# Exp straight from the score PSUM, a check of the row sums in place of the max pass, and another access order for the query copies, in a grouped-query attention kernel

## The chip, the cores and the metric

The kernel runs on one core of a Trainium2 chip. The metric is the time of one execution on the device in microseconds (us), and lower is better. "Median" is the median of several executions. The "span" is the length of the one execution that the profiler recorded; in these runs it is 1.7 to 3.6 us shorter than the time of that same execution. Some executions are flagged slow: they lie over 1.5% above the fastest of their kernel.

## The reference, cut to what matters

```python
B, Hq, Hkv, Sq, Sk, D = 16, 32, 8, 16, 2048, 128
# q, k, v: bfloat16, normal * 0.05
k = jnp.repeat(k, rep, axis=1)          # rep = Hq // Hkv = 4
v = jnp.repeat(v, rep, axis=1)
scores = jnp.einsum("bhqd,bhkd->bhqk", q, k) * D ** -0.5
p = softmax(scores, axis=-1)
return jnp.einsum("bhqk,bhkd->bhqd", p, v)
```

There are 128 heads of K and V (16 batches times 8). Each serves 4 x 16 = 64 rows of queries. The kernel works on pairs of heads, so that a tile has 128 rows, and there are 64 pairs. A pair needs two heads of K and two of V, 512 KB each. In all the core moves 138.43 MB by its data queue. The inputs are small, so the scores lie near zero and every row sum of the exponentials lies near 2048.

## The kernel before: the parts that matter

The kernel is a static program. A list scheduler in Python, run while the kernel is built, puts the operations of each engine in an order, from a table of durations. On the chip nothing is decided any more: each engine runs its list in order and waits on semaphores. In the code and the views PE is TensorE, PEld its loading of weights, DVE VectorE, ACT ScalarE, POOL GpSimd, and SPq the queue of SyncE that issues the DMA transfers. Names that end in _ps lie in PSUM, the memory that TensorE writes its results to; the other tiles lie in SBUF.

```python
# operations of pair p (engine): what each waits for
# kx  DVE       KT <- Kn      transposes K in 32x32 blocks      (K landed)
# qt  PE        QT_ps <- Qr   transposes a quarter of a chunk of queries
# qe  ACT       QT <- QT_ps   copies it out, interleaving the rows
# S   PE        S_ps <- KT,QT scores, 128 x 2048 f32, one buffer
# mx  DVE       Sneg <- S_ps  negate, scale, and take the row minimum on the way
# ex  ACT       P <- Sneg     exp with the bias nbias; its accumulator is the row sum
# pt  PE        PT_ps <- P    two halves; pe (ACT or DVE) copies each out
# pv  PE        O_ps <- PT,V
# rc, nm, ST    1/rowsum, scaling, store
add(("S", p), ("kx", 2 * p), ("kx", 2 * p + 1), ..., opt(p >= 1, ("mx", p - 1)))
add(("mx", p), ("S", p), opt(p >= 2, ("ex", p - 2)))
add(("ex", p), ("mx", p), ...)
...
_ENGS = {"kx": ("dve",), "mx": ("dve",), "nm": ("act", "dve"), "pe": ("act", "dve"), "qe": ("act",), ...}
...
elif kind == "mx":
    ins = eng.tensor_scalar(Sneg[p % 2][:, :], S_ps[:, :], -scale, None,
                            op0=ALU.mult, op1=ALU.min, accum_out=nbias[:, p:p + 1])
elif kind == "ex":
    ins = eng.activation(P[...], Sneg[p % 2][...], ACT.Exp,
                         bias=nbias[:, p:p + 1], scale=-1.0, accum_out=rowsum[:, p:p + 1])
...
if kind == "qe":                      # NI = 8
    dst = QT[p % 2][:, op[2], :].rearrange("d (a i) -> d i a", i=NI)   # store: step of 8 bf16 = 16 bytes
    src = QT_ps[:, 0:qch].rearrange("d (i a) -> d i a", i=NI)          # read: one after the other
ins = eng.activation(dst, src, ACT.Copy) if me == "act" else eng.tensor_copy(dst, src)
```

A chunk of queries serves eight pairs and needs four copies "qe". All loads and stores stand in one queue, in order; K runs two pairs ahead of V.

Of the kernel before, what the change touches and what calls it, by code (L numbers as in the profile page):

```python
# [6 lines left out]
ALU = mybir.AluOpType  # L7
# [5 lines left out]
NBV = 14  # L13
# [6 lines left out]
QLEAD = 5  # L20

# [4 lines left out]
    ("dve", "pe"): 0.69, ("act", "pe"): 1.03, ("act", "qe"): 1.06, ("act", "nm"): 0.42,  # L26
# [10 lines left out]
         "qe": ("act",), "qr": ("pool",), "ex": ("act",), "qt": ("pe",), "S": ("pe",), "pt": ("pe",), "pv": ("pe",)}  # L37
# [3 lines left out]
def make_ops(NP, pairs_per_chunk):  # L41
# [23 lines left out]
    for p in range(NP):  # L65
        add(("S", p), ("kx", 2 * p), ("kx", 2 * p + 1), *[("qe", ch(p), x) for x in range(4)],
            opt(p >= 1, ("mx", p - 1)))
        add(("mx", p), ("S", p), opt(p >= 2, ("ex", p - 2)))
        add(("ex", p), ("mx", p), *[opt(p >= 2, ("pt", p - 2, h)) for h in range(2)])
        for h in range(2):  # L70
            add(("pt", p, h), ("ex", p), opt(p >= 1, ("pe", p - 1, h)))
            add(("pe", p, h), ("pt", p, h), opt(p >= NPT, ("pv", p - NPT)))
        add(("pv", p), ("pe", p, 0), ("pe", p, 1), ("V", 2 * p), ("V", 2 * p + 1), opt(p >= 1, ("nm", p - 1)))
        add(("rc", p), ("ex", p))
        add(("nm", p), ("pv", p), ("rc", p), opt(p >= NBO, ("ST", p - NBO)))
        add(("ST", p), ("nm", p))
# [20 lines left out]
def build_schedule(NP, pairs_per_chunk):  # L97

    deps, dma = make_ops(NP, pairs_per_chunk)
# [51 lines left out]
def bass_standalone__gqa_softmax__sampling_kernel(  # L151
# [36 lines left out]
    rowsum = sb("rowsum", [128, NP], F32)  # L188
    rrec = sb("rrec", [128, NP], F32)
# [8 lines left out]
    sem_eng = {e: sem(f"sem_{e}") for e in ("pe", "dve", "act", "pool")}  # L198
    rings = {"K": NBK, "V": NBV, "Q": 2, "ST": NBO}
    sem_dma = {kind: [sem(f"sem_{kind}{i}") for i in range(n)] for kind, n in rings.items()}  # L200

    deps, progs, _ = build_schedule(NP, qch // 128)
    where = {}
    for e in ("pe", "dve", "act", "pool"):
        for i, op in enumerate(progs[e]):
            where[op] = (e, i + 1)
# [6 lines left out]
    def wait_point(op):  # L213
        if op[0] in rings:
            n = rings[op[0]]
            return sem_dma[op[0]][op[1] % n], 16 * (op[1] // n + 1)
        e, i = where[op]
        return sem_eng[e], i

    def make_waiter(eng, me):  # L220
        seen = {}

        def waits(op):
            need = {}
            for d in deps[op]:
                if me == "pe" and d in where and where[d][0] == "pe":
                    continue
                s, n = wait_point(d)
                key = s.name
                if n > max(seen.get(key, 0), need.get(key, (None, 0))[1]):  # L230
                    need[key] = (s, n)
            for key, (s, n) in need.items():
                seen[key] = n
                eng.wait_ge(s, n)

        return waits

    def elementwise(eng, me):
        waits = make_waiter(eng, me)
        for op in progs[me]:  # L240
# [12 lines left out]
            elif kind == "ex":  # L253
                ins = eng.activation(  # L254
                    P[p % 2][:, :].rearrange("m (r a j) -> m a r j", a=4, j=32),
                    Sneg[p % 2][:, :].rearrange("m (a r j) -> m a r j", a=4, j=32), ACT.Exp,
                    bias=nbias[:, p:p + 1], scale=-1.0, accum_out=rowsum[:, p:p + 1])
            elif kind == "rc":
                ins = eng.reciprocal(rrec[:, p:p + 1], rowsum[:, p:p + 1])  # L259
            elif kind == "nm":  # L260
                dst, src, r = Osb[p % NBO][:, :], O_ps[:, 0:128], rrec[:, p:p + 1]
                if me == "act":
                    ins = eng.activation(dst, src, ACT.Copy, scale=r)  # L263
                else:
                    ins = eng.tensor_scalar(dst, src, r, None, op0=ALU.mult)  # L265
            else:
                if kind == "qe":
                    dst = QT[p % 2][:, op[2], :].rearrange("d (a i) -> d i a", i=NI)
                    src = QT_ps[:, 0:qch].rearrange("d (i a) -> d i a", i=NI)
                else:  # L270
                    h = op[2]
                    dst = PT[p % NPT][:, 8 * h:8 * (h + 1), :]
                    src = PT_ps[h][:, :].rearrange("k (t m) -> k t m", t=8)
                ins = eng.activation(dst, src, ACT.Copy) if me == "act" else eng.tensor_copy(dst, src)  # L274
            ins.then_inc(sem_eng[me], 1)

    with nc.Block() as block:  # L277

        @block.gpsimd
        def _(gp):  # L280
            gp.iota(iota_t[:, :], [[1, 128]], base=0, channel_multiplier=-1).then_inc(sem_id, 1)
            gp.wait_ge(sem_id, 1)
            gp.tensor_scalar(ident[:, :], iota_t[:, :], 0.0, None, op0=ALU.is_equal).then_inc(sem_id, 1)
            elementwise(gp, "pool")

        @block.sync
        def _(sp):
            waits = make_waiter(sp, "sp")
            for op in progs["sp"]:
                kind, x = op  # L290
                waits(op)
                s = x % rings[kind]
                if kind == "K":
                    dst, src = Kn[s][:, :].bitcast(BF16), kf[x].rearrange("(a j) d -> a (j d)", j=J)
                elif kind == "V":
                    dst, src = Vb[s][:, :, :], vf[x].rearrange("(a j) d -> a j d", j=J)
                elif kind == "Q":
                    dst, src = Qn[s][:, :, :], qf[qch * x:qch * (x + 1), :].rearrange("(a i) d -> a i d", i=NI)
                else:
                    dst, src = of[128 * x:128 * (x + 1), :], Osb[s][:, :]  # L300
                sp.dma_start(dst, src).then_inc(sem_dma[kind][s], 16)  # L301
            for p in range(max(0, NP - NBO), NP):
                sp.wait_ge(*wait_point(("ST", p)))

        @block.tensor
        def _(pe):
            waits = make_waiter(pe, "pe")
            pe.wait_ge(sem_id, 2)
            for op in progs["pe"]:
                kind, p = op[0], op[1]  # L310
                waits(op)
                if kind == "qt":
                    x = op[2]
                    for i in range(NI):
                        ins = pe.transpose(  # L315
                            QT_ps[:, 128 * i:128 * (i + 1)],
                            Qr[:, x, i, :],
                            ident[:, :],
                        )
                elif kind == "S":  # L320
                    c, pp = divmod(p, qch // 128)
                    for x in range(4):
                        for a in range(4):
                            for gg in range(2):
                                kt = KT[p % NKT][32 * a:32 * (a + 1), gg, :].bitcast(BF16)
                                kt = kt.rearrange("i (r b j e) -> i r b j e", b=2, j=32, e=2)
                                ins = pe.matmul(  # L327
                                    S_ps[64 * gg:64 * (gg + 1), 512 * a:512 * (a + 1)],
                                    QT[c % 2][32 * a:32 * (a + 1), x, 128 * pp + 64 * gg:128 * pp + 64 * (gg + 1)],
                                    kt[:, :, x // 2, :, x % 2],  # L330
                                    start=(x == 0), stop=(x == 3), tile_position=(32 * a, 64 * gg),
                                )
                elif kind == "pt":
                    h = op[2]
                    for t in range(8):
                        r = 8 * h + t
                        ins = pe.transpose(PT_ps[h][:, 128 * t:128 * (t + 1)],  # L337
                                           P[p % 2][:, 128 * r:128 * (r + 1)], ident[:, :])
                else:
                    for r in range(J):  # L340
                        for gg in range(2):
                            ins = pe.matmul(  # L342
                                O_ps[64 * gg:64 * (gg + 1), 0:128],
                                PT[p % NPT][:, r, 64 * gg:64 * (gg + 1)],
                                Vb[(2 * p + gg) % NBV][:, r, :],
                                start=(r == 0), stop=(r == J - 1), skip_group_check=True,
                            )
                ins.then_inc(sem_eng["pe"], 1)

        @block.vector  # L350
        def _(dve):
            elementwise(dve, "dve")

        @block.scalar
        def _(act):
            elementwise(act, "act")
# [28 lines left out]
```

## Time and profile before

| | before |
|---|---|
| median of the first three runs | 478.08 us (477.15 to 480.02) |
| span of the profiled run | 473.1 us |
| busiest engine | ScalarE (ACT), 381.1 us, 81% |
| copies QT<-QT_ps | 32 x 4.72 us = 151 us |
| max passes Sneg<-S_ps | 64 x 2.29 us = 147 us |
| data moved, mean rate | 138.43 MB, 293 GB/s |

The first view is the page of the kernel before: first the busy time of each engine, then, for 40 equal slices of the span (11.8 us each), the granted TensorE clock in tenths, the busy share of the DMA engines in tenths and what they moved.

```profile
PE 275.6 (58%) x5376; PEld 194.3 (41%) x5376; DVE 327.2 (69%) x369; ACT 381.1 (81%) x308; POOL 28.9 (6%) x34
...
PEclk9999877975898677966899667995579776779999
DMA  8951978995889549995599839998299972999990
GB/s 300 413 220 49 348 265 286 360 413 182 308 315 401 197 169 407 352 361 182 213 406 400 319 133 332 340 408 306 89 353 320 401 278 115 340 337 363 411 367 10
```

The DMA row is not flat. It stands at 9 for a few slices and then falls, again and again, as one chunk of queries follows another (GB/s 49, 182, 169, 182, 133, 89, 115). In many of the slices at or after a fall the granted TensorE clock is low as well (digits 5 to 7).

The groups of instructions of the kernel before name the operations. The columns are: source line, engine, operation, output<-input, shapes, count; then total busy us and mean ns of one; then the idle time before them and who ended it.

```profile
L251 DVE TENSOR_SCALAR_CACHE_REDUCE Sneg<-S_ps 128x2048 f32<-128x2048 f32 x64 | 146.5, 2289 | 66.2 <-PE S_ps L327 64.1
L274 ACT ACTIVATE QT<-QT_ps 128x1024 bf16<-128x1024 bf16 x32 | 151.1, 4723 | 13.5 <-PE QT_ps L315 13.4
L254 ACT ACTIVATE P<-Sneg,nbias 128x2048 bf16<-128x2048 f32 x64 | 129.3, 2020 | 8.8 <-DVE Sneg L251 8.6
L274 ACT ACTIVATE PT<-PT_ps 128x1024 bf16<-128x1024 bf16 x92 | 94.9, 1072 | 31.2 <-PE PT_ps L337 31.2
```

The second and the last of these lines are the ones to compare. Both are ScalarE copies of 1024 bf16 elements for each of 128 partitions out of PSUM. One takes 4.72 us, the other 1.07 us. What differs between them is the engine's access pattern. The first line is the max pass.

The windows view of the kernel before gives busy us of PE, PEld, DVE, ACT and POOL in a stretch of 10 us, with the granted clock, the DMA's share and GB/s at the end. The first stretch lies at a chunk of queries, the second does not.

```profile
220.00:230.00 10.00, 7.44 (x96) 5.47 (x96) 5.85 (x7) 9.24 (x9) 0.00 (x0) 0.53 0.05 11
440.00:450.00 10.00, 6.36 (x163) 4.55 (x160) 9.91 (x11) 8.99 (x11) 0.00 (x0) 1.00 1.03 412
```

At the chunk ScalarE is busy for 9.24 of 10 us, and the DMA falls to 11 GB/s; the granted clock is 0.53 there and 1.00 in the other stretch. Away from the chunk the DMA runs at 412 GB/s.

This is the longest of the waits of the transfer queue (total us, times, longest us):

```profile
SPq L301 <- ACT O L263: 257.6, 53, 26.2
```

The queue waits for the scaling of an output tile. Only a store waits for that, and the store of a pair stands in the same queue in front of later loads. From 215.0 to 228.2 us, for example, nothing is issued: ScalarE runs two query copies of 4.7 us (started at 213.78 and 220.18), then the scaling ends at 228.14 us and the store goes out at 228.16. Waits for a free buffer of K (<-DVE KT) come to 2.1 us in all.

### The profile page before, as it was taken

Reading aid. Unit: us, or ns where it says so; the run is one execution under the profiler, and the core shown is the slowest. Engines: PE = TensorE matmul, PEld = TensorE weight load, DVE = VectorE, ACT = ScalarE, POOL = GpSimd, SP = SyncE. Lnnn points to the kernel's source line nnn. Section 1 sums busy time; section 2 is a strip of 40 time slices with the busy share of each in tenths; the row PEclk is TensorE's granted clock in tenths of the full one; section 3 lists DMA queues with packets and bytes.
Section 4 is the critical chain, followed back from the end, with each engine's and each line's share of the span. In section 5 each row is a group of like instructions: output and inputs, shape, how many; then the busy total and the mean of one; then the engine's idle time right before and its main releaser. Section 6 shows DMA issues by size and latency. Waiting matters only on the chain.

```text
span 473.1 us, 11999 instructions
## 1 busy us (share of the span) xinstructions
PE 275.6 (58%) x5376; PEld 194.3 (41%) x5376; DVE 327.2 (69%) x369; ACT 381.1 (81%) x308; POOL 28.9 (6%) x34
## 2 busy tenths in 40 slices
PE   1147547737655566646666456654666645675754
PEld 1115435525443354433544234442544424454543
DVE  5237567936795478955799366993579645889994
ACT  6859987999499966999588993899948799479894
POOL 0200000300003000110003000030000300000000
PEclk9999877975898677966899667995579776779999
DMA  8951978995889549995599839998299972999990
GB/s 300 413 220 49 348 265 286 360 413 182 308 315 401 197 169 407 352 361 182 213 406 400 319 133 332 340 408 306 89 353 320 401 278 115 340 337 363 411 367 10
DMA packets 47282, 139.19 MB, mean 294 GB/s; under 512 B 13440, under 2 KB 13440, under 8 KB 47232
## 3 DMA queue, kind: packets, MB, share of 16 engines
q1 hardware_dynamic: 47232, 138.43, 77.9%
q8 instruction: 42, 0.69, 0.6%
q14 instruction: 8, 0.07, 0.0%
HBM read 136.31 MB, written 2.10 MB: 293 GB/s over the span
## 4 chain that ended last, share of the span: by engine, by line
issue 16%; ACT 14%; PE 12%; DVE 4%; DMA 3%; POOL 1%; SPq 1%; ACTq 0%; POOLq 0%
ACT PT L274 7%; ACT QT L274 5%; PE S_ps L327 4%; PE O_ps L342 4%; PE PT_ps L337 3%; DMA Qn<-in_q_dram 3%; ACT P L254 2%; DVE Sneg L251 1%; DVE PT L274 1%; POOL Qr L249 1%; DVE KT L244 1%; PE QT_ps L315 1%; SPq L301 1%; ACTq L277 0%; ACT O L263 0%
## 5 line engine op out<-in xcount | busy, mean ns | idle before, releaser
L251 DVE TENSOR_SCALAR_CACHE_REDUCE Sneg<-S_ps 128x2048 f32<-128x2048 f32 x64 | 146.5, 2289 | 66.2 <-PE S_ps L327 64.1
L274 ACT ACTIVATE QT<-QT_ps 128x1024 bf16<-128x1024 bf16 x32 | 151.1, 4723 | 13.5 <-PE QT_ps L315 13.4
L244 DVE STREAM_TRANSPOSE KT<-Kn 128x1024 int32<-128x1024 int32 x128 | 153.5, 1225 | 2.4 <-DMA Kn<-in_k_dram 2.3
L254 ACT ACTIVATE P<-Sneg,nbias 128x2048 bf16<-128x2048 f32 x64 | 129.3, 2020 | 8.8 <-DVE Sneg L251 8.6
L342 PE MATMUL O_ps<-Vb,PT 128*64 128x128 bf16 x2048 | 82.6, 243 | 77.1 <-ACT PT L274 69.8
L274 ACT ACTIVATE PT<-PT_ps 128x1024 bf16<-128x1024 bf16 x92 | 94.9, 1072 | 31.2 <-PE PT_ps L337 31.2
L342 PEld LDWEIGHTS O_ps<-Vb,PT 128*64 128x64 bf16 x2048 | 71.2, 125 | 92.6 <-ACT PT L274 81.9
L327 PE MATMUL S_ps<-KT,QT 32*64 32x512 bf16 x2048 | 89.5, 469 | 21.3 <-DVE KT L244 13.7
L337 PE MATMUL PT_ps<-ident,P 128*128 128x128 bf16 x1024 | 84.4, 248 | 11.8 <-ACT P L254 11.6
L337 PEld LDWEIGHTS PT_ps<-ident,P 128*128 128x128 bf16 x1024 | 72.2, 113 | 40.5 <-ACT P L254 29.0
L315 PE MATMUL QT_ps<-ident,Qr 128*128 128x128 bf16 x256 | 27.0, 270 | 84.6 <-ACT QT L274 56.7
L315 PEld LDWEIGHTS QT_ps<-ident,Qr 128*128 128x128 bf16 x256 | 20.4, 120 | 93.0 <-issue 77.6
L327 PEld LDWEIGHTS S_ps<-KT,QT 32*64 32x64 bf16 x2048 | 30.7, 120 | 49.8 <-issue 20.7
L249 POOL COPY Qr<-Qn 128x1024 bf16<-128x1024 bf16 x28 | 28.0, 1040 | 347.9 <-DMA Qn<-in_q_dram 346.7
L274 DVE COPY PT<-PT_ps 128x1024 bf16<-128x1024 bf16 x36 | 24.1, 689 | 32.1 <-PE PT_ps L337 32.0
L263 ACT ACTIVATE O<-O_ps,rrec 128x128 bf16<-128x128 f32 x53 | 20.9, 394 | 30.6 <-PE O_ps L342 30.3
L259 DVE RECIPROCAL rrec<-rowsum 128x1 f32<-128x1 f32 x64 | 9.1, 143 | 24.7 <-ACT P L254 24.6
L265 DVE TENSOR_SCALAR O<-O_ps,rrec 128x128 bf16<-128x128 f32 x11 | 3.9, 351 | 14.8 <-PE O_ps L342 14.8
L254 ACT ACTIVATION_READ_ACCUMULATOR P<-Sneg,nbias 128x1 f32 x64 | 12.5, 195 | 0.0
L251 DVE DVE_READ_ACCUMULATOR Sneg<-S_ps 128x1 f32 x64 | 5.3, 83 | 0.0
L249 DVE COPY Qr<-Qn 128x1024 bf16<-128x1024 bf16 x2 | 1.3, 690 | 3.4 <-DMA Qn<-in_q_dram 3.4
L249 ACT ACTIVATE Qr<-Qn 128x1024 bf16<-128x1024 bf16 x2 | 2.0, 1050 | 1.4 <-DMA Qn<-in_q_dram 1.4
(7 smaller groups left out, 2.5 us busy)
## 6 DMA issues: line engine op xcount, KB each, us to landing
Kn<-in_k_dram SPq DMA_DIRECT2D x128, 512.0 KB, 6.4
Vb<-in_v_dram SPq DMA_DIRECT2D x128, 512.0 KB, 8.0
Qn<-in_q_dram SPq DMA_DIRECT2D x8, 256.0 KB, 6.1
out_dram<-O SPq DMA_DIRECT2D x64, 32.0 KB, 4.7
```

The source lines that it names most:

```text
L244: ins = eng.transpose(KT[(p // 2) % NKT][:, p % 2, :], Kn[p % NBK][:, :])
L249: ins = eng.activation(dst, src, ACT.Copy) if me == "act" else eng.tensor_copy(dst, src)
L251: ins = eng.tensor_scalar(Sneg[p % 2][:, :], S_ps[:, :], -scale, None, op0=ALU.mult, op1=ALU.min, accum_out=nbias[:, p:p + 1])
L254: ins = eng.activation(P[p % 2][:, :].rearrange("m (r a j) -> m a r j", a=4, j=32), Sneg[p % 2][:, :].rearrange("m (a r j) -> m a r j", a= ...
L259: ins = eng.reciprocal(rrec[:, p:p + 1], rowsum[:, p:p + 1])
L263: ins = eng.activation(dst, src, ACT.Copy, scale=r)
L274: ins = eng.activation(dst, src, ACT.Copy) if me == "act" else eng.tensor_copy(dst, src)
L301: sp.dma_start(dst, src).then_inc(sem_dma[kind][s], 16)
L315: ins = pe.transpose(QT_ps[:, 128 * i:128 * (i + 1)], Qr[:, x, i, :], ident[:, :],)
L327: ins = pe.matmul(S_ps[64 * gg:64 * (gg + 1), 512 * a:512 * (a + 1)], QT[c % 2][32 * a:32 * (a + 1), x, 128 * pp + 64 * gg:128 * pp + 64 * ...
L337: ins = pe.transpose(PT_ps[h][:, 128 * t:128 * (t + 1)], P[p % 2][:, 128 * r:128 * (r + 1)], ident[:, :])
L342: ins = pe.matmul(O_ps[64 * gg:64 * (gg + 1), 0:128], PT[p % NPT][:, r, 64 * gg:64 * (gg + 1)], Vb[(2 * p + gg) % NBV][:, r, :], start=(r ...
```

## The change

The intent was to drop the pass that finds the row maximum. Softmax does not need it where exp can neither overflow nor vanish, so exp reads the scores straight from PSUM. For safety the kernel tests at its end that all row sums lie in 1e-18..1e18. If one does not, every engine runs a second, complete program with the max pass. The diff also turns the access order of the query copy round, and lets that copy run on VectorE too.

```diff
-         "qe": ("act",), ...
+         "qe": ("act", "dve"), ...
@@ dependencies
-            opt(p >= 1, ("mx", p - 1)))
-        add(("mx", p), ("S", p), opt(p >= 2, ("ex", p - 2)))
-        add(("ex", p), ("mx", p), ...)
+            opt(p >= 1, ("mx" if general else "ex", p - 1)))
+        if general:
+            add(("mx", p), ("S", p), opt(p >= 2, ("ex", p - 2)))
+        add(("ex", p), ("mx" if general else "S", p), ...)
@@ exp
+                src = Sneg[p % 2] if prog.general else S_ps
...
-                    bias=nbias[:, p:p + 1], scale=-1.0, accum_out=rowsum[:, p:p + 1])
+                    bias=nbias[:, p:p + 1] if prog.general else 0.0, scale=-1.0 if prog.general else scale,
+                    accum_out=rowsum[:, p:p + 1])
@@ query copy
-                    dst = QT[p % 2][:, op[2], :].rearrange("d (a i) -> d i a", i=NI)
-                    src = QT_ps[:, 0:qch].rearrange("d (i a) -> d i a", i=NI)
+                    dst = QT[p % 2][:, op[2], :].rearrange("d (a i) -> d a i", i=NI)
+                    src = QT_ps[:, 0:qch].rearrange("d (i a) -> d a i", i=NI)
@@ the end of each engine's program
+    def unless_in_range(eng, work):
+        reg = eng.alloc_register("flag")
+        eng.wait_ge(sem_flag, 4)
+        eng.reg_load(reg, flag[0:1, 0:1].bitcast(I32))
+        with eng.If_ne(reg, all_within):
+            fast.wait_stores(eng)
+            work()                      # the whole second program
@@ VectorE, after its last operation
+            for x, (bound, test) in enumerate(((LOW, ALU.is_ge), (1.0 / LOW, ALU.is_le))):
+                dve.tensor_scalar(inside[:, x, :], rowsum[:, :], bound, None, op0=test, op1=ALU.add,
+                                  accum_out=within[:, x:x + 1]).then_inc(sem_flag, 1)
+            dve.wait_ge(sem_flag, 3)    # PE has summed the counts over the partitions
+            dve.reduce_sum(flag[0:1, 0:1], QT_ps[0:1, 0:4].bitcast(F32), ...).then_inc(sem_flag, 1)
```

Since the scheduler runs again, the orders change too: 19 of the 32 query copies, 72 of the 128 PT copies (before: 36) and 58 of the 64 scalings (before: 11) now stand on VectorE.

## The prediction

> **What bounds the kernel now.** By the page's busy table ScalarE is the busiest (381.1 of 473.1 us, 81%), then VectorE (327.2), TensorE (275.6, mean clock 0.825). The groups of instructions say why: 32 copies of transposed queries, QT<-QT_ps, take 4723 ns each (151.1 us), while PT<-PT_ps, with as many elements and bytes, takes 1072 ns. Their store steps by 16 bytes per bf16 element. [...] These copies come in fours. The 40-slice table shows the damage: around each chunk of queries the DMA falls from 400–413 GB/s to 100–250 and PEclk to 0.5–0.7, and the first score matmul starts only at 28.1 us (timeline). Between chunks most 10-us windows show 390–412 GB/s, PEclk 1.0. There the timeline shows a pair of heads every 4.7 us when data is at hand, ScalarE full (exp 2.0 + 0.2, two PT copies 1.94, O 0.36).
>
> **What the change does.** It removes the 64 max passes (2289 ns + 83 = 151.8 us of VectorE) and their place in the chain S -> max -> exp. Exp reads PSUM; PT copies from PSUM (1072 ns) cost what a same-sized SBUF copy costs on ScalarE (1050), so I expect 2.0 + 0.2 us still. S_ps is now held until exp ends, so score and exp of adjacent pairs no longer overlap. The query copy's store becomes contiguous, its PSUM read strided. Instruction order moves work to VectorE: 19 of 32 query copies, 72 of 128 PT copies (was 36), 58 of 64 O scalings (was 11).
> Sums from the trace's durations, query copy assumed 1.1 us on ScalarE, 1.25 on VectorE:
> - ScalarE 64x2.2 + 56x1.05 + 13x1.1 + 6 = 220 us;
> - VectorE 128x1.225 + 72x0.69 + 58x0.35 + 64x0.14 + 19x1.25 + 1 = 261 us;
> - TensorE, warm, per pair 1.08 (S) + 1.07 (PT) + 1.08 (O).
> The serial chain of a pair, exp 2.2 -> PT_ps 1.07 -> S 1.08 -> waits 0.4, is 4.75 us.
>
> **The new bound is the DMA.** 138.43 MB at the saturated 402 GB/s (estimate: mean of the full windows of before) is 344 us, 5.35 us a pair, above the chain's 4.75 and every engine's sum. [...] the trace never passes 413. Add 3 us of ramp, about 4 for the last O, scaling and store, and 3–4 for the check at the end (two tests, a matmul, a reduction, register load, branch), partly under the store; then 2–4 for the difference between span and timed run. The fallback does not execute: every row sum should be near 2048.
>
> **Predicted: 358 us**, 350 to 380 eight times in ten; faster by over 2% 0.97, within 2% 0.02, slower 0.01.
>
> **What would show it.** DMA share near 99% in almost all slices without hollows at chunks; PEclk near 1.0; no Sneg group; QT copies 1.0–1.3 us; exp from PSUM 2.0–2.1 us; engines at about 220 (ScalarE) and 260 (VectorE); first S near 13 us; last load landing near 347 us.
>
> **What would make it wrong.** Strided PSUM reads still costing 4 us: three such copies per chunk on VectorE would push it above 5.35 us a pair (375–390 us). Exp from PSUM much slower than 2.2 us, or TensorE throttled to half clock (chain 2.2 + 2x2.15 + 0.4 = 6.9 us), would make the S–exp chain the bound. In-order stores in the load queue could stall loads early. The branch at the end could cost more than 4 us.

344 us of transfers, 3 of ramp, about 4 for the last output, 3 to 4 for the check and 2 to 4 between span and timed run come to 356 to 359 us, put at 358. Two figures had no figure of the trace behind them and were guesses: 1.25 us for a query copy on VectorE, and 3 to 4 us for the check. The runs later showed 1.19 and 3.5 us. Between span and timed run the profiled execution has 1.8 us before (474.86 - 473.1) and 1.8 after (358.22 - 356.4). "Warm" stands for a granted clock of 1.00: there the trace before has 1.08 us for the scores of a pair (start at 442.76 us), and 1.93 us in a stretch at 0.53 (start at 222.15 us).

## The result and the profile after

The changed kernel takes 359.4 us in the median of 4 runs (357.52 to 360.96), against 478.79 us for the kernel before in the same rounds. The ratio is 0.7506, with a 95% interval of 0.7456 to 0.7557. Here and below a ratio is the mean time of one kernel's fast runs over that of the other's fast runs of the same rounds, so it is not quite the ratio of the medians. The output is correct, and the second program did not run.

This is the page of the changed kernel, with the same rows as before (a slice is now 8.9 us).

```profile
PE 240.3 (67%) x5378; PEld 173.7 (49%) x5378; DVE 244.2 (69%) x348; ACT 201.1 (56%) x206; POOL 28.9 (8%) x35
...
PEclk9999998998989998989988998999989999989897
DMA  7999999999999999999999999999999999999940
GB/s 291 413 409 407 410 411 406 412 411 411 409 411 410 411 412 410 411 412 409 410 409 412 411 410 409 411 409 409 411 411 410 405 410 404 408 412 410 405 164 12
```

The DMA row is 9 from the second slice to the 38th. No fall is left. No engine of computation is busy for more than 69% of the span.

The groups of instructions after the change:

```profile
L255 DVE STREAM_TRANSPOSE KT<-Kn 128x1024 int32<-128x1024 int32 x128 | 157.5, 1232 | 14.1 <-DMA Kn<-in_k_dram 13.6
L266 ACT ACTIVATE P<-S_ps 128x2048 bf16<-128x2048 f32 x64 | 120.1, 1877 | 54.9 <-PE S_ps L326 54.7
L287 ACT ACTIVATE PT<-PT_ps 128x1024 bf16<-128x1024 bf16 x56 | 57.3, 1023 | 76.9 <-PE PT_ps L336 76.9
L287 DVE COPY PT<-PT_ps 128x1024 bf16<-128x1024 bf16 x72 | 47.4, 667 | 7.4 <-PE PT_ps L336 7.1
L287 DVE COPY QT<-QT_ps 128x1024 bf16<-128x1024 bf16 x19 | 22.7, 1194 | 1.6 <-PE QT_ps L314 1.6
L287 ACT ACTIVATE QT<-QT_ps 128x1024 bf16<-128x1024 bf16 x13 | 13.2, 1019 | 5.4 <-PE QT_ps L314 5.4
```

The query copies fell from 4723 to 1019 ns on ScalarE, and take 1194 ns on VectorE. Exp takes 1877 ns. The max pass has no line.

The chain of waits that ended last, by engine, for the changed kernel:

```profile
DMA 62%; PE 19%; ACT 8%; SPq 5%; DVE 4%; issue 2%
```

Followed back from the end, 62% of the span is waiting for a transfer. The kernel before had 3% there, but its chain could be followed over about half of its span only (its shares add up to 51%).

The windows view of the changed kernel, with one long stretch and one at the end of the stream of loads:

```profile
43.00:335.00 292.00, 202.35 (x4570) 146.47 (x4564) 206.09 (x290) 168.32 (x174) 23.93 (x24) 0.94 1.03 410
338.00:345.00 7.00, 4.58 (x122) 2.99 (x121) 4.35 (x7) 2.89 (x4) 0.00 (x0) 1.00 0.56 215
```

For 292 us the DMA moves 410 GB/s. This is the new bound. Near 338 us the DMA's busy share falls to about half, and stays there for about 7 us, before the loads are through.

The last view is the timeline of the changed kernel from 22.9 us, where data is at hand. Its columns are start, duration, engine, line, operation.

```profile
22.93 1.07 PE L336 MATMUL PT_ps<-ident,P 128*128 128x128 bf16 x16 [0.54 <-ACT P L266]
23.92 1.14 PE L326 MATMUL S_ps<-KT,QT 32*64 32x512 bf16 x32
25.14 1.88 ACT L266 ACTIVATE P<-S_ps 128x2048 bf16<-128x2048 f32 x1 [0.44 <-PE S_ps L326]
27.16 1.07 PE L336 MATMUL PT_ps<-ident,P 128*128 128x128 bf16 x16 [0.53 <-ACT P L266]
```

The transposes of P start at 22.93 and again at 27.16 us. The serial chain exp, PT, S takes 4.2 us a pair, when nothing makes it wait.

### The profile page after: what moved, and what is told of

It is laid out like the page before. It is cut to its first block, busy times and chain, and to the rows that moved or that the text cites. A ratio compares the mean times of both kernels' runs of the same rounds, so it can differ in the third digit from the quotient of the medians.

```text
span 356.4 us, 11923 instructions
## 1 busy us (share of the span) xinstructions
PE 240.3 (67%) x5378; PEld 173.7 (49%) x5378; DVE 244.2 (69%) x348; ACT 201.1 (56%) x206; POOL 28.9 (8%) x35
## 4 chain that ended last, share of the span: by engine, by line
DMA 62%; PE 19%; ACT 8%; SPq 5%; DVE 4%; issue 2%
DMA Vb<-in_v_dram 58%; PE O_ps L341 7%; ACT P L266 6%; PE PT_ps L336 6%; SPq L304 5%; PE S_ps L326 4%; DMA Kn<-in_k_dram 3%; DVE KT L255 2%; DVE PT L287 1%; ACT QT L287 1%; PE QT_ps L314 1%; DMA Qn<-in_q_dram 1%; DVE O L278 1%; ACT Qr L260 0%; DVE rrec L272 0%
## 5 line engine op out<-in xcount | busy, mean ns | idle before, releaser
L255 DVE STREAM_TRANSPOSE KT<-Kn 128x1024 int32<-128x1024 int32 x128 | 157.5, 1232 | 14.1 <-DMA Kn<-in_k_dram 13.6
L266 ACT ACTIVATE P<-S_ps 128x2048 bf16<-128x2048 f32 x64 | 120.1, 1877 | 54.9 <-PE S_ps L326 54.7
L341 PE MATMUL O_ps<-Vb,PT 128*64 128x128 bf16 x2048 | 74.1, 227 | 81.6 <-DMA Vb<-in_v_dram 59.6
L287 ACT ACTIVATE PT<-PT_ps 128x1024 bf16<-128x1024 bf16 x56 | 57.3, 1023 | 76.9 <-PE PT_ps L336 76.9
L336 PE MATMUL PT_ps<-ident,P 128*128 128x128 bf16 x1024 | 77.5, 234 | 13.4 <-ACT P L266 13.2
L326 PE MATMUL S_ps<-KT,QT 32*64 32x512 bf16 x2048 | 77.2, 410 | 1.2 <-ACT QT L287 1.2
L287 DVE COPY PT<-PT_ps 128x1024 bf16<-128x1024 bf16 x72 | 47.4, 667 | 7.4 <-PE PT_ps L336 7.1
L278 DVE TENSOR_SCALAR O<-O_ps,rrec 128x128 bf16<-128x128 f32 x58 | 20.2, 348 | 43.5 <-PE O_ps L341 43.4
L287 DVE COPY QT<-QT_ps 128x1024 bf16<-128x1024 bf16 x19 | 22.7, 1194 | 1.6 <-PE QT_ps L314 1.6
L287 ACT ACTIVATE QT<-QT_ps 128x1024 bf16<-128x1024 bf16 x13 | 13.2, 1019 | 5.4 <-PE QT_ps L314 5.4
L266 ACT ACTIVATION_READ_ACCUMULATOR P<-S_ps 128x1 f32 x64 | 12.4, 194 | 0.0
L276 ACT ACTIVATE O<-O_ps,rrec 128x128 bf16<-128x128 f32 x6 | 2.2, 367 | 6.5 <-PE O_ps L341 6.5
## 6 DMA issues: line engine op xcount, KB each, us to landing
Vb<-in_v_dram SPq DMA_DIRECT2D x128, 512.0 KB, 13.5
```

The costliest lines, as they stand in the source:

```text
L255: ins = eng.transpose(KT[(p // 2) % NKT][:, p % 2, :], Kn[p % NBK][:, :])
L266: ins = eng.activation(P[p % 2][:, :].rearrange("m (r a j) -> m a r j", a=4, j=32), src[:, :].rearrange("m (a r j) -> m a r j", a=4, j=32) ...
L276: ins = eng.activation(dst, src, ACT.Copy, scale=r)
L278: ins = eng.tensor_scalar(dst, src, r, None, op0=ALU.mult)
L326: ins = pe.matmul(S_ps[64 * gg:64 * (gg + 1), 512 * a:512 * (a + 1)], QT[c % 2][32 * a:32 * (a + 1), x, 128 * pp + 64 * gg:128 * pp + 64 * ...
L336: ins = pe.transpose(PT_ps[h][:, 128 * t:128 * (t + 1)], P[p % 2][:, 128 * r:128 * (r + 1)], ident[:, :])
```

## The experiments

The theory after the result had two parts. First, the slow query copies made the hollows in the DMA before. Second, the DMA is the floor after. The rival was that the max pass, or its place in the chain from S to exp, was what had cost the time. Twelve kernels were run, on the chip, beside the kernel before. All give the right result unless said.

### The access order alone

```diff
# kernel before
-  dst = QT[...].rearrange("d (a i) -> d i a", i=NI); src = QT_ps[...].rearrange("d (i a) -> d i a", i=NI)
+  dst = QT[...].rearrange("d (a i) -> d a i", i=NI); src = QT_ps[...].rearrange("d (i a) -> d a i", i=NI)
```

> The kernel before with one change: the query copy writes its tile contiguously and reads PSUM strided, as the changed kernel does. Max pass, instruction order and engines stay as before. Theory (the slow query copies made the hollows, and the DMA is the floor): QT copies fall from 4.72 to about 1.02 us on ScalarE, 32x3.7 = 118 us of ScalarE go, ScalarE lands near 264 us and VectorE stays near 327 us, a pair takes 4.7 us plus 0.5 us of query copies, just under the DMA's 5.3 us: 358 to 372 us. Rival (the max pass and its place in the chain S -> max -> exp was what cost the time): well above 400 us.

Measured: 373.41 us median of 4 runs, ratio 0.7837 (0.7779 to 0.7896). The instructions and their orders are those of the kernel before. These two lines alone are worth 106 of the 119 us. The page of this run:

```profile
PE 247.3 (67%) x5376; PEld 174.8 (47%) x5376; DVE 325.6 (88%) x369; ACT 267.8 (72%) x308; POOL 28.9 (8%) x34
...
GB/s 286 414 409 409 410 408 411 409 411 411 411 397 398 406 354 368 413 348 399 396 327 411 369 412 367 385 415 272 392 400 356 402 396 412 369 396 413 410 247 7
```

The rival falls. But the range was missed by a little, and the two rows say where the theory was loose. VectorE is busy for 88% of the span, more than ScalarE, and the DMA has dents (272 to 370 GB/s in single slices, from the 15th on). So this kernel does not stand at the DMA's pace only.

### The removal of the max pass without the new access

```diff
# changed kernel
-  dst = QT[...].rearrange("d (a i) -> d a i", i=NI); src = QT_ps[...].rearrange("d (i a) -> d a i", i=NI)
+  dst = QT[...].rearrange("d (a i) -> d i a", i=NI); src = QT_ps[...].rearrange("d (i a) -> d i a", i=NI)
```

> The changed kernel with the old access of the query copy put back (strided store); 13 of the 32 copies run on ScalarE, 19 on VectorE. Theory: the ScalarE copies cost 4.7 us again; what the strided store costs VectorE no trace shows. If VectorE pays as much (4 us and up), three of them a chunk push it above the DMA's pace: 375 to 420 us. If VectorE pays nothing (about 1.2 us), only one slow copy a chunk is left, and the time stays at 360 to 368 us. Rival (the max pass was the cost): 358 to 362 us whatever the copies take.

Measured: 401.32 us, ratio 0.8426 (0.8357 to 0.8496). The groups of the query copies in this run:

```profile
L287 DVE COPY QT<-QT_ps 128x1024 bf16<-128x1024 bf16 x19 | 89.4, 4706 | 9.4 <-PE QT_ps L314 9.4
L287 ACT ACTIVATE QT<-QT_ps 128x1024 bf16<-128x1024 bf16 x13 | 61.6, 4735 | 8.2 <-PE QT_ps L314 8.2
```

The strided store costs VectorE as much as ScalarE, 4.71 against 4.74 us. So the cost is not that of one engine alone.

The same with the query copies kept on ScalarE, as they were before:

```diff
# the run above
-         "qe": ("act", "dve"), ...
+         "qe": ("act",), ...
```

> As the run before it, with the query copies kept on ScalarE as in the kernel before: the removal of the max pass alone. Theory: 32 copies of 4.7 us in fours with PE waiting for each, hollows in the DMA at each chunk: 410 to 460 us. Rival (the max pass was the cost): 358 to 375 us.

Measured: 406.93 us, ratio 0.8544 (0.8485 to 0.8603), a little below the range of the theory and far from that of the rival. As in every run of the changed kernel the scheduler ran again: 71 of the 128 PT copies and 56 of the 64 scalings stand on VectorE here. The page still has the hollows (284, 249, 278, 282 GB/s) at the chunks, and the slow copies:

```profile
GB/s 307 412 368 12 284 249 357 369 412 412 409 278 350 415 409 359 326 391 403 400 317 289 409 401 400 282 334 412 401 361 300 373 405 393 330 317 377 412 294 13
...
L287 ACT ACTIVATE QT<-QT_ps 128x1024 bf16<-128x1024 bf16 x32 | 152.8, 4774 | 4.8 <-PE QT_ps L314 4.8
```

The runs put together, with the ratio to the kernel before:

| | old access of the query copy | new access |
|---|---|---|
| with the max pass | 1 | 0.7837 |
| without it | 0.8544 on ScalarE, 0.8426 on both engines | 0.7506 |

The two gains do not add. Alone the access gains 0.216 and the removal 0.146 to 0.157; together they gain 0.249, not 0.36 to 0.37. (The cell at the lower right lets VectorE take query copies; without the max pass, the new access with the copies on ScalarE alone was not run.) Something else stops the time near 359 us.

### Less data

```diff
# one V transfer for each pair; both heads multiply with it (wrong result on purpose)
-            dma += [("V", 2 * (t - DV)), ("V", 2 * (t - DV) + 1)]
+            dma += [("V", 2 * (t - DV))]
-        add(("pv", p), ..., ("V", 2 * p), ("V", 2 * p + 1), ...)
+        add(("pv", p), ..., ("V", 2 * p), ...)
-                            Vb[(2 * p + gg) % NBV][:, r, :],
+                            Vb[(2 * p) % NBV][:, r, :],
```

In the changed kernel:

> The changed kernel with only one V transfer for each pair (both heads use the first head's V: wrong result on purpose, same work on every engine), so 105 instead of 138 MB. Theory (DMA is the floor, 5.35 us a pair at 411 GB/s): the floor falls to 1.6 MB a pair = 3.9 us, the chain exp 2.0 -> PT 1.07 -> S 1.1 of 4.2 us a pair becomes the bound, 64x4.2 + 25 = 285 to 305 us. Rival (the chain through the single score buffer or VectorE already sets the pace): 350 us or more.

Measured: 304.43 us in the median, ratio 0.6385 (0.6332 to 0.6437), at the upper end of the theory's range; one of the four runs was slow. The number of products, exps and copies is as before, 33.5 MB fewer move, and the time falls by 55 us. That shows that the DMA is the bound of the changed kernel. The busy times and the chain of this run:

```profile
PE 222.9 (74%) x5378; PEld 161.5 (54%) x5378; DVE 256.4 (85%) x391; ACT 159.6 (53%) x163; POOL 28.9 (10%) x35
...
PE 41%; ACT 32%; DMA 15%; issue 4%; SPq 3%; POOL 2%; DVE 1%; DVEq 0%
```

The chain no longer runs over transfers of V but over exp, S and PT: TensorE and ScalarE hold 73% of it. This is the next bound, at 301.2 / 64 = 4.7 us a pair, start and end included, with VectorE at 85% close behind. One thing is not held fixed: the scheduler, given fewer transfers, put all PT copies and scalings on VectorE and all query copies on ScalarE.

The same cut in the kernel before with the new access, where the max pass is kept:

> The kernel before with the new access of the query copy and only one V transfer for each pair (wrong result on purpose), so 105 MB: the max pass is kept, the DMA floor is lowered. The changed kernel with the same cut took 304 us. Theory (with the whole V both stand at the DMA's pace, and the max pass's removal is worth only what the full DMA leaves of it): here the engines set the pace, ScalarE 264 us and VectorE 327 us of work at about 5.1 us a pair, so 340 to 365 us, 35 to 60 us more than the changed kernel with the same cut, where the gap with the whole V was 14 us. Rival (the gap of 14 us is a fixed cost of start and end): 310 to 325 us.

Measured: 368.35 us, ratio 0.7701 (0.7643 to 0.7758), 3 us over the range of the theory. The page:

```profile
PE 246.2 (67%) x5376; PEld 173.3 (47%) x5376; DVE 326.1 (89%) x370; ACT 266.6 (73%) x307; POOL 28.9 (8%) x34
...
GB/s 270 415 313 324 356 192 351 361 293 250 245 339 328 334 202 293 340 291 370 235 241 374 206 368 210 339 335 224 379 183 359 322 259 395 195 308 345 301 69 9
```

This run moves 33.5 MB less than the run of the access alone, and is only 5 us faster. So that kernel was not bound by the DMA in the main, as I had assumed for it, but by its engines. VectorE is busy for 326.1 us here, 5.1 us a pair. The other 41 us of the span, up to 366.7 / 64 = 5.7 us a pair, VectorE waits; its longest waits are for scores (17.0 us in all). That its fixed order makes these waits is likely, and was not tested. The gap that the max pass makes is 64 us where the data is cut (368.35 against 304.43), and 14 us where it is whole (373.41 against 359.4; by the ratios, 0.7837 against 0.7506, it is 16). The removal, with the new order that comes with it, is worth 64 us to the engines. The DMA's floor lets 14 to 16 of them through.

### How wide a store has to be

```diff
# changed kernel: the four copies of a chunk write 1, 2, 4, 8 neighbours at a time
+  per = (1, 2, 4, 8)[op[2]]
+  dst = QT[p % 2][:, op[2], :].rearrange("d (a h l) -> d h a l", h=NI // per, l=per)
+  src = QT_ps[:, 0:qch].rearrange("d (h l a) -> d h a l", h=NI // per, l=per)
```

> The changed kernel, in which the four query copies of a chunk write their tiles in four orders: 1, 2, 4 and 8 neighbouring bf16 elements[...] at a time (the result stays right, and the PSUM reads are strided in all four). Theory A [...]: 4.7, 2.4, 1.2 and 1.0 us on ScalarE. Theory B [...]: 4.7, then 1.0 to 1.1 us for the other three. VectorE should show the same steps from 4.7 us, down to 1.2 us.

In theory A the cost falls with the number of neighbours written together (estimate, 4.7 us / 1024 = 4.6 ns for each separate piece); in theory B two neighbours are enough.

Each order stands on its own source line here: lines 285, 287 and 291 are 1, 2 and 8 neighbours (4 neighbours took 1019 ns on ScalarE and 1188 on VectorE). The groups:

```profile
L285 ACT ACTIVATE QT<-QT_ps 128x1024 bf16<-128x1024 bf16 x7 | 33.3, 4757 | 0.5 <-PE QT_ps L323 0.5
L287 ACT ACTIVATE QT<-QT_ps 128x1024 bf16<-128x1024 bf16 x2 | 2.2, 1088 | 1.4 <-PE QT_ps L323 1.4
L291 ACT ACTIVATE QT<-QT_ps 128x1024 bf16<-128x1024 bf16 x2 | 2.0, 1019 | 1.2 <-PE QT_ps L323 1.2
L285 DVE COPY QT<-QT_ps 128x1024 bf16<-128x1024 bf16 x1 | 4.7, 4697 | 0.0
L287 DVE COPY QT<-QT_ps 128x1024 bf16<-128x1024 bf16 x6 | 7.4, 1226 | 5.0 <-PE QT_ps L323 5.0
L291 DVE COPY QT<-QT_ps 128x1024 bf16<-128x1024 bf16 x6 | 7.1, 1185 | 0.0
```

On both engines the step is between one and two neighbours: 4757 to 1088 ns on ScalarE, 4697 to 1226 ns on VectorE. After that it hardly falls. Theory A falls, and what theory B expected came out: two neighbouring elements at a time are enough. Why they are is not shown. Every slow store here writes single bf16 elements, 2 bytes each, 16 bytes apart. Single elements at another step would tell whether it is the lone element or the step that costs, and were not run. (With 1 neighbour the read from PSUM is contiguous, and not strided as the text above says, so the slow copies owe nothing to the read.) The read from PSUM is strided by 256 bytes in the last line of each engine, and that costs ScalarE nothing (1019 ns, against 1023 for a contiguous PT copy of the changed kernel). VectorE takes 1185 ns there, against 667 for a contiguous PT copy.

### The end of the kernel: what the check costs

Four kernels were timed on one chip beside each other. The first is the changed kernel again.

> The changed kernel once more, as the yardstick for the three runs beside it on the same chip: 357 to 362 us, ratio to before near 0.751. Both theories of the tail expect the same here.

Measured: 357.88 us, ratio 0.7506 (0.7471 to 0.7541).

```diff
# no check, no second program
-            unless_in_range(...)             # on all five engines
-            (two tests, matmul, reduction)
```

> The changed kernel without the check of the row sums and without the second program. In the changed kernel 5.9 us pass from the end of the last O scaling to the end of the span, in the kernel before 2.3 us. Theory (that difference is the whole cost of the check): 3 to 4 us less than the changed kernel, about 1%. Rival (the check hides under the last store, and the longer end comes from something else, for example the longer program): less than 1 us.

Measured: 355.51 us, ratio 0.7447 (0.7412 to 0.7482).

```diff
# the check stays; what is skipped is short
         with eng.If_ne(reg, all_within):
             fast.wait_stores(eng)
-            work()
```

> The changed kernel with the check and the branch kept, but the body that is skipped holds only its eight waits instead of a whole second program. Theory (the register load and the two tests cost, the length skipped does not): within 0.7 us of the changed kernel. Rival [...]: 2 us or more below the changed kernel, near the run without a check.

The rival put the cost on the length of the body that is jumped over.

Measured: 355.6 us, ratio 0.7445 (0.741 to 0.7479). My theory for this run falls, and the rival holds: with a short body to skip, the kernel with the check takes what the kernel without it takes. The intervals of these ratios overlap by a little, so the 2.3 us in the medians are not sure to the last tenth, but the single runs lie apart (357.26 to 360.06 us, against 354.13 to 356.53). The end of each trace is sharper. This is the line of the span and of one of the instruction queues (packets, MB) of the changed kernel, and then, from its timeline, its last scaling:

```profile
span 355.5 us, 11923 instructions
...
q14 instruction: 12, 0.10, 0.1%
```

```profile
349.22 0.35 DVE L278 TENSOR_SCALAR O<-O_ps,rrec 128x128 bf16<-128x128 f32 x1 [1.18 <-PE O_ps L341]
```

And of the run with the short body:

```profile
span 354.5 us, 11923 instructions
...
q14 instruction: 8, 0.07, 0.0%
```

```profile
351.77 0.35 DVE L278 TENSOR_SCALAR O<-O_ps,rrec 128x128 bf16<-128x128 f32 x1 [1.18 <-PE O_ps L341]
```

From the end of the last scaling to the end of the span it takes 355.5 - 349.57 = 5.9 us with the long body, and 354.5 - 352.12 = 2.4 us with the short one. The run without a check takes 354.4 - 352.12 = 2.3 us, and the kernel before 2.3 us. So the tests, the register load and the branch add 0.1 us to the end (2.4 against 2.3 us), and the other 3.5 us (5.9 - 2.4) come with the length of what is jumped over. (The spans of these two executions differ by 1.0 us only, because with the short body the last scaling itself came 2.6 us later. In that execution the PV product that starts at 341.98 us took 1.92 us; the same product took 1.08 us, from 340.91, in the one with the long body.) The queue for instructions moved 12 packets with the long body (14 in the first profile of the changed kernel) and 8 with the short one. What the extra packets carried, and whether the 3.5 us are a wait for them, was not shown.

### A shorter end

```diff
# each PV product is queued one pair later on PE
+        add(("pv", p), ..., ("S", p + 2))       # the last but one: after ("pt", p + 1, 1)
```

> Of the run with the shorter end, the order of PE alone; the check stays where the changed kernel has it. Theory: 4 to 5 us less than the changed kernel (about 355 us), the last PV product ending within 2 us of the landing of the last V. Rival: no gain.

Measured on another chip: 357.36 us, ratio 0.7492 (0.7452 to 0.7531). The gain is not clear of noise, and the expected 4 to 5 us are not there. The other half of the theory held: the last V lands at 347.11 us, and the last PV product ends at 348.35.

```diff
# the order above, and
+            if op == ("rc", NP - 1): (the two tests, on VectorE)
+            if op == ("pt", NP - 1, 1): (the matmul that sums the counts, on PE)
+            (count and register load on VectorE before the last scaling; register load on SP before the last store)
```

> The changed kernel with a shorter end: each PV product is queued one pair later on PE (behind S of the pair after next), so that scores, exp and transposes of the last pairs no longer wait behind a product that waits for its V; the row-sum tests run right after the last reciprocal, the count before the last PV product, and the register loads before the last scaling and the last store. Theory (DMA is the floor and only the end can still be cut: the last V lands near 343 us and the last PV product ends at 350.1): 5 us from the order, 1 to 3 us from the check, so 351 to 355 us. Rival (what follows the last load is a chain that the order can't shorten, or the later products delay the stores that stand in the load queue): 358 us or more.

Measured beside the changed kernel: 354.44 us, ratio 0.7434 (0.7401 to 0.7467) against 0.7506 (0.7471 to 0.7541). The intervals do not meet, so this version beats both kernels, by 1% of the changed one. The last steps of its chain of waits, with start, us and what:

```profile
335.30 11.74 DMA Vb<-in_v_dram
347.04 0.14 issue
347.18 1.10 PE O_ps L362 x32
348.30 0.35 DVE O L281
```

The last PV product starts right when the last V lands, at 347.04 us. I had taken the end of the 410 GB/s stretch, plus a little, as the landing (343 us). The loads really end near 347 us (346.8 in the first profile of the changed kernel: issue at 333.36 and 13.5 us to landing), since the last 7 us run at half the DMA's share. So the order had little left to gain, in this run as in the one before: the last scaling ends at 348.65 us here and at 348.72 with the order alone, against 349.57 in the changed kernel beside it. In the traces the check's new places do the rest: from there to the end of the span it takes 3.9 us here, and 5.9 us in the other two. What halves the DMA's busy share at the end (0.56 from 338 to 345 us, against 1.03 before) is open. The packed trace of the changed kernel has 16 packets or more in flight at 336 us and 8 to 11 from 340 to 344 us, but it does not say which engine moved what.

### Does the second program work?

```diff
-LOW = 1e-18
+LOW = 1e4
```

> The changed kernel with the lower bound set to 1e4, which every row sum (near 2048) fails, so that the second program runs on every engine. The result must stay right. The second program is the run of the access alone in all but its first loads, so the span should be the changed kernel's 356 us plus about 370 us: 720 to 735 us. If the fallback were broken, the result would be wrong or the run would hang.

Measured: right result, 725.01 us in one run, span 723.2 us. Both forms of exp ran:

```profile
L266 ACT ACTIVATE P<-Sneg,nbias 128x2048 bf16<-128x2048 f32 x64 | 128.1, 2002 | 10.0 <-DVE Sneg L262 9.9
L266 ACT ACTIVATE P<-S_ps 128x2048 bf16<-128x2048 f32 x64 | 120.1, 1877 | 59.7 <-PE S_ps L326 59.6
```

The first load of the second program starts at 353.93 us, so the second program takes 369 us, and the run of the access alone has a span of 370.5 us. The safe path works, and costs about twice the time when it is needed.

## Why the prediction was right

**The total.** Predicted 358 us, 350 to 380; measured 359.4 us. Right.

**What bounded the kernel before.** The prediction put it on ScalarE and its 4.7 us copies. Right: the two lines of access alone bring 479 to 373 us. How the copies reach the DMA it left open; the queue's waits show it (257.6 us behind stores that wait for their scaling). It named stores in the load queue only as a risk for the changed kernel. The first scores, at 28.1 us before and expected near 13, start at 13.4. In one place the reading was wrong. Between chunks I called ScalarE full at 4.7 us a pair. The windows view says 8.99 of 10 us for ScalarE and 9.91 for VectorE, so there VectorE was the full engine. It did not matter to the predicted time, but it made me expect the run of the access alone to sit at the DMA's pace, and it sits nearer to VectorE's (88% busy).

**What the copies would cost.** Assumed 1.1 and 1.25 us, measured 1.02 and 1.19. Right. The first stood near the 1.07 us of the PT copy; the second was a guess, since the only copies of this size on VectorE in the trace before were contiguous, at 0.69 us. That the store pattern makes the 4.7 us was argued from the trace before and is shown by the runs: with 2, 4 or 8 neighbours in place of 1, ScalarE takes 1.09, 1.02 and 1.02 us for 4.76, and VectorE 1.23, 1.19 and 1.19 for 4.70. Why a single element costs so much is not shown.

**Engine sums.** Predicted 220 us for ScalarE and 261 for VectorE; the page has 201 and 244. The durations were near (VectorE's groups add up to 260 us: 157.5 + 47.4 + 20.2 + 9.9 + 22.7 + 1.3 + about 1). The page's busy time counts the overlap of neighbouring instructions once, so a sum of means overstates it. For ScalarE exp was also shorter, 1.88 us and not 2.0. The forced second program has 2002 ns with a bias for each partition and 1877 without it, 125 ns apart. But the source of the two differs too (SBUF and PSUM), so which of the two makes the difference is not shown.

**The chain.** Predicted 4.75 us a pair, measured 4.2. The waits and exp were oversized. It stayed below the DMA's pace, as said.

**The DMA as the new bound.** Right: a share of 9 in nearly all slices, 62% of the last chain, and 55 us less when 33.5 MB are taken away. The rate was sized too low (402, measured 410 GB/s), and the end of the stream was not foreseen (7 us at half share). At 410 GB/s the bytes take 338 us and not 344, and half the rate for 7 us costs about 3.5 us (estimates from these two figures). So the errors cancel in large part: the last load was predicted for about 347 us, and lands at 346.8 in the changed kernel and at 347.04 in the run with the shorter end. This part was right by luck in its terms. PEclk was not quite "near 1.0": it is 0.94 in the mean.

**The end.** 3 to 4 us, partly under the store, were set aside for the check. Measured 3.5 us in the trace and about 2.3 in the medians, but from the jump over the second program. The tests, the register load and the branch itself, which I had listed, add 0.1 us.

**The fall-back case in "what would make it wrong".** I wrote 375 to 390 us for slow copies on both engines, from 4 us a copy. That case was run, as the access undone, where a copy takes 4.7 us, and it takes 401 us, so the range there was too low (the one given before that run, 375 to 420 us, holds it). That the slow copies also block what stands behind them in the static order is the likely reason, but it was not tested alone.

## What to carry to other kernels

When a change has several parts, run each part alone: here the part that gave the change its name is worth about 15 us on top of the other, and the two swapped access patterns alone are worth 106. Compare copies of equal size in the groups of instructions; where one takes 4.4 times as long as its twin, as here, look at its store pattern; here it was enough to write two neighbouring bf16 elements at a time, in place of single ones 16 bytes apart (4.76 to 1.09 us on ScalarE, 4.70 to 1.23 on VectorE). Ask of a queue that runs in order what stands in front of the loads. Before counting on two gains together, work out the floor under both, from the bytes and the best rate that the trace itself shows.
